# Three edits to a fused attention, gating and token-mixing kernel on one Trainium2 core: last output chunk in two single PSUM banks, ninth blocks' group third, strided operands loaded at earlier steps

## The chip, the cores and the metric

One Trainium2 chip, one core of it. The metric is the device time of one launch in microseconds (us), the median of several runs, lower being better. Engines are named as in the profile: PE is TensorE, DVE VectorE, ACT ScalarE, POOL GpSimd, and SP the engine that issues almost all DMAs.

## The reference

Four batches of 576 rows go through three stages, all with float32 inputs and outputs.

```python
# 1. attention, 8 heads of 64; heads 0-3 local, heads 4-7 strided
scores = q @ k.T / 8
mask_local   = (rel >= 0) & (rel < 32)
mask_strided = (rel >= 0) & (pos_k % 32 == pos_q % 32)
x = softmax(where(mask, scores, -1e9)) @ v          # -> [4, 576, 512]
# 2. spatial gating
h = relu(x @ w_in); u, v = h[..., :512], h[..., 512:]
v_n = (v - mean(v)) / sqrt(var(v) + 1e-6)
x = (u * (w_spatial @ v_n + b_spatial)) @ w_out
# 3. mixing by angles
theta = x @ w_theta
y = w_tok_r @ (x * cos(theta)) + w_tok_i @ (x * sin(theta))
u = x + y
out = u + relu(u @ w_ch)
```

## The kernel before, in words

The matrix products of stages 2 and 3 run in float16 in three passes (high by high, high by low, low by high), over 128x128 weights and 288 columns, two such halves per tile of 128x576. For each batch the main chain is: `v` (240 products in all), its mean and variance (tile `rs` on DVE), the normalised `vn`; `u`; `sp` (the spatial product, which reads `vn`); `x`, the product with `w_out`; `th`, the product with `w_theta`; `z_chunk`, which turns an angle tile of PSUM into sines and cosines (tile `ta`, on ACT and DVE) and has them transposed by DMA into `zf`; `y`, the product with the token weights; `c`, the last product. Generators (`main_v`, `main_mid`, `main_end`) issue it in pieces.

PSUM has three two-bank tiles for this chain (pool `ps_m`, `bufs=3`, function `pm`, line 202) and two single banks, `sc` and `av` (pool `ps_a`, function `pa`, line 205), for attention. A product that wants a fourth `pm` tile waits until the oldest has been read: of the four angle tiles of a batch, the last waits for the reads of the first.

Attention of batches 0 to 2 is computed in float32 in nine groups of score blocks (list `groups`, line 423): a local group holds up to four blocks of 64 rows by 96 keys, one further local group holds the ninth block of both local head pairs, and four strided groups hold six (the last four) blocks of 64 by 64. A group goes through steps: scores on PE into `sc` (`gr_scores`), shift by the maximum on DVE (`gr_shift`, `TENSOR_REDUCE st<-sc`, `TENSOR_TENSOR sm<-sc,st`), exponential on ACT (`gr_exp`), transposes (`gr_turn`), product with the values (`gr_pv`), transposes back and copies into `xT` as a float16 pair (`gr_out`, ACT for the high part, DVE for the low part). Batch 0 runs alone at the start (`attention0`), each group in a pair of banks (`at`, or `sc` and `av`), four pairs in rotation. Batches 1 and 2 (`attention1`, line 661) run beside the main chain of the batch before, one step at a time. Batch 3 (`attention`) uses float16.

In `attention1` a table `loads` (line 680) says after which step's scores the operands of the strided head pairs are loaded: `load_a` loads queries and keys into `kt`, the buffer that a local pair used, and `load_b` loads the values. SP issues all of them in one queue.

Weights arrive as float64 and are made into float16 pairs on the way: a staging buffer is filled by DMA, ACT and DVE form a float32 (`ACTIVATE zf<-zf`, `ACTIVATE wx<-zf`, `SCALAR_TENSOR_TENSOR wx<-zf,wx`), ACT copies the high part (`wtok<-wx`), POOL subtracts for the low part. The token weights (`tok_part`) come in five pieces, i = 0, 2, 4, 6, 8, through two staging buffers in turn, `xT` and `zf`, so that a piece is loaded when the piece two before it has left the buffer. `w_spatial`'s last rows and the bias (`sp_tail`, tile `wspt`) are scaled by ACT and DVE.

In the main chain and in attention of batches 1 to 3 a scheduler sets the order of instructions on each engine by its own costs, from program order with some operations (`ha`, `hv`) put 200 places forward; each engine, and SP's queue, then runs its list in that order.

The end of the last batch (`main_end`, line 989): output chunks 2 and 3 get a `pm` tile each; the last three products of chunk 3 are done for the left half and then for the right half of the columns, each followed by a relu on ACT, an add on DVE and a store.

Of the kernel before, what the change touches and what calls it, by code (L numbers as in the profile page):

```python
# [17 lines left out]
AF = mybir.ActivationFunctionType  # L18
# [9 lines left out]
PS = WS * XS  # L28
# [37 lines left out]
def kernel(  # L66
# [24 lines left out]
    class Pinned:  # L91


        def __init__(self, name):
            self.name, self.engine = name, getattr(tc.nc, name)
# [24 lines left out]
    B, DM, S = out.shape  # L120
    P = 128
# [4 lines left out]
    HS = S // 2  # L126
# [18 lines left out]
    hv, ha, hg = Ahead(nc.vector, AHEAD), Ahead(nc.scalar, AHEAD), Ahead(nc.gpsimd, AHEAD)  # L145
# [56 lines left out]
    def pm(name):  # L202
        return ps_m.tile([P, 2, 512], F32, tag="pm", name=name)

    def pa(tag):
        return ps_a.tile([P, 512], F32, tag=tag, name=tag)
# [4 lines left out]
    def halves(ps):  # L211
        return ps[:, :, 0:HS]

    def fold(ap):
        return ap.rearrange("p (a c) -> p a c", a=2)
# [197 lines left out]
    def spans_of(u):  # L413
        spans = []
        for i, hp, blk, r0, R, o, t0 in pv_blocks(u):
            if spans and spans[-1][0] == hp:
                spans[-1][3] += R
            else:
# [1 line left out]
        return spans  # L420

    QB, CB = 64, 54
    groups = [(True, [(hp, blk) for blk in range(b0, b0 + 4)]) for hp in range(2) for b0 in (0, 4)]
    groups += [(True, [(0, 8), (1, 8)]),
               (False, [(2, i) for i in range(6)]), (False, [(2, i) for i in range(6, 11)] + [(3, 10)]),
               (False, [(3, i) for i in range(6)]), (False, [(3, i) for i in range(6, 10)])]
    NG = len(groups)

    def load_qk(b, hp, q, k, c0, c1, by=None):
        by = by or nc.sync  # L430
        local = hp < 2
        src = kzl[b, hp] if local else kzs[b, hp - 2]
        k0, k1 = (c0 + STRIDE if c0 else 0, c1 + STRIDE) if local else (c0, c1)
        by.dma_start(q[:, c0:c1], qp[b, hp][:, c0:c1])
        for j in range(2):
            h = slice(64 * j, 64 * j + 64)
            by.dma_start(k[h, k0:k1], src[h, j, k0:k1])
# [104 lines left out]
    def gr_exp(g, sm):  # L542
        n = len(groups[g][1]) * (96 if groups[g][0] else QB)
        nc.scalar.activation(sm[:, 0:n], sm[:, 0:n], AF.Exp, scale=0.125)
# [116 lines left out]
    def attention1(b):  # L661
        q, k, v = {}, {}, {}

        def load_a(hp):
            q[hp], k[hp] = kts[hp % 2][:, 0], kts[hp % 2][:, 1]
            load_qk(b, hp, q[hp], k[hp], 0, S)

        def load_b(hp):
            v[hp] = att_p.tile([P, 9, VW], F32, tag="vT", name="v32", bufs=2)
            if hp < 2:  # L670
                load_vl(b, hp, v[hp])
            else:
                load_vs(b, v[hp][:, 0:6].unsqueeze(1), (hp,))

        load_a(0)
        load_b(0)
        yield
        load_a(1)
        load_b(1)
        loads = {4: (load_a, 2), 6: (load_b, 2), 7: (load_b, 3)}  # L680
        un, xs = {}, {}
        for s in range(NG + 3):
            if s < NG:
                sm = att_p.tile([P, 384], F32, tag="sm", name="sm", bufs=2)
                pT = att_p.tile([P, 4, P], F32, tag="pT", name="pT32", bufs=2)
                st = att_p.tile([P, 2, 6], F32, tag="st", name="st", bufs=4)
                un[s] = (sm, pT, st)
            if s >= 3:
                gr_out(b, s - 3, xs.pop(s - 3), pa("sc"))
            if 2 <= s < NG + 2:  # L690
                sm, pT, st = un.pop(s - 2)
                pv = pa("av")[:, 0:3 * VW].rearrange("p (i n) -> p i n", i=3)
                gr_pv(s - 2, v, pT, pv, st, pT)
                xs[s - 2] = pT
            if s < NG:
                sm, pT, st = un[s]
                sc = pa("sc")
                gr_scores(s, q, k, sc)
                gr_shift(s, sc, sm, st)
                gr_exp(s, sm)  # L700
            if s in loads:
                f, hp = loads[s]
                f(hp)
                if s == 4:
                    load_a(3)
            if 1 <= s <= NG:
                sm, pT, st = un[s - 1]
                gr_turn(s - 1, sm, pa4("av"), pT)
            yield
# [279 lines left out]
    def main_end(b):  # L989

        def tok_evac(m, ps):
            x = x2f[:, m, :]
            hv.scalar_tensor_tensor(fold(x), halves(ps), 1.0 / WS, fold(x), op0=ALU.mult, op1=ALU.add)
            split((x2h[:, 0, m, 0:S], x2h[:, 1, m, 0:S]), x, H[E_YLO[m + 4 * (b > 0)]], E_YHI[m + 4 * (b > 0)])

        for m in range(NC):
            ps = pm(f"y{m}")
            rounds = [(i, PASS) for i in range(NZ)]
            if m == 0 and b == B - 1:

                rounds = [(i, ((0, 0), (0, 1))) for i in range(NZ)] + [(i, ((1, 0),)) for i in range(NZ)]
            for k, (i, passes) in enumerate(rounds):
                for n, (ze, we) in enumerate(passes):
                    mm2(ps, zz[:, i, ze, m * P:(m + 1) * P], wtok[:, we, i, :],
                        k == 0 and n == 0, k == len(rounds) - 1 and n == len(passes) - 1)
                if k == len(rounds) - 1:
                    tok_evac(m, ps)
                if k % 3 == 2:
                    yield


        for m0 in (0, 2):
            tiles = [pm(f"c{m0 + i}") for i in range(2)]
            for cs in ((0, 1, 2), (3,)):
                for i in range(2):
                    m = m0 + i
                    o = s1("o") if cs[0] == 3 else None
                    parts = ((0,), (1,)) if cs[0] == 3 and m == NC - 1 and b == B - 1 else ((0, 1),)
                    for a in parts:
                        for c in cs:  # L1020
                            for n, (we, xe) in enumerate(PASS):
                                mm2(tiles[i], wch[:, we, c, m * P:(m + 1) * P], x2h[:, xe, c, :],
                                    c == 0 and n == 0, c == NC - 1 and n == 2, part=a)
                        if cs[0] == 3:
                            f = slice(a[0] * HS, (a[-1] + 1) * HS)
                            h = slice(a[0], a[-1] + 1)
                            ha.activation(fold(o)[:, h], halves(tiles[i])[:, h], AF.Relu, scale=1.0 / PS)
                            hv.scalar_tensor_tensor(o[:, f], x2f[:, m, f], 1.0 / XS, o[:, f], op0=ALU.mult, op1=ALU.add)
                            nc.sync.dma_start(out[b, m * P:(m + 1) * P, f], o[:, f])
                    yield  # L1030


    def switch():
        early[0] = False
# [44 lines left out]
    l0, a0, b0, c0, e0 = win_steps(1, 0)  # L1079
# [115 lines left out]
```

## Time and profile before

| | |
|---|---|
| median of 3 runs | 504.88 us |
| lowest and highest | 504.08, 508.08 us |
| the profiled execution, its own time | 506.96 us |
| span from its first to its last instruction | 505.1 us |
| PE busy in that span | 485.1 us (96%) |
| DVE, ACT, POOL busy | 284.8, 267.8, 92.9 us |

PE is busy for nearly the whole span, so the time is PE's work plus the short stretches in which PE stands still. The views to read are therefore those of PE's waits and, around each wait, the timeline of the other engines. The clock that the throttle granted to PE is given per stretch, 1.00 being full speed (2.4 GHz) and 0.50 half.

### The profile page before, as it was taken

To read this page: it belongs to the slowest core of one execution; us is meant where nothing else is said; L and a number is where in the kernel's file an instruction comes from. 1 tells how busy PE (TensorE), PEld (TensorE's weight loads), DVE (VectorE), ACT (ScalarE), POOL (GpSimd) and SP (SyncE) were. 2 spreads that over 40 slices of the span, in tenths; PEclk is the share of its full clock that TensorE was granted. 3 is DMA by queue.
4 is the path that set the end of the run, shared out by engine and by line. 5 is a ranking of instruction groups with operands and counts; after the bars stand their busy time and mean duration, and the time that the engine had idled before them with its cause. 6 is when DMAs were issued, how large, how long until landed. Compare 5 with 4: busy or idle time off the path is not lost. (4 is left out here: it accounts for less than half of the span.)

```text
span 505.1 us, 10834 instructions
## 1 busy us (share of the span) xinstructions
PE 485.1 (96%) x4460; PEld 364.4 (72%) x4460; DVE 284.8 (56%) x607; ACT 267.8 (53%) x475; POOL 92.9 (18%) x91
## 2 busy tenths in 40 slices
PE   7889989998999999999999989999999999999996
PEld 5655757776567777888758867777657777777774
DVE  3765986555699343473499578772587121227412
ACT  2657788587994233345672757754862022149202
POOL 2042147225124400021003210021005200210220
PEclk9999999999899999999999999999999999999999
DMA  6868748377691024221080156230160020003402
GB/s 177 279 203 234 260 151 270 103 185 225 188 223 49 1 66 150 72 80 27 1 185 4 31 128 195 47 60 5 38 151 1 1 95 1 0 2 80 111 1 93
DMA packets 71788, 52.72 MB, mean 104 GB/s; under 512 B 50552, under 2 KB 59960, under 8 KB 71738
## 3 DMA queue, kind: packets, MB, share of 16 engines
q1 hardware_dynamic: 71434, 51.42, 36.5%
q8 instruction: 35, 0.57, 0.5%
q10 hardware_dynamic: 304, 0.61, 0.4%
q14 instruction: 15, 0.12, 0.1%
HBM read 35.36 MB, written 4.72 MB: 79 GB/s over the span
## 5 line engine op out<-in xcount | busy, mean ns | idle before, releaser
L103 PE MATMUL y<-wtok,zf 128*128 128x288 f16 x864 | 107.2, 286 | 1.0 <-DMA zf<-vn 1.0
L103 PEld LDWEIGHTS <-zf 128*128 128x128 f16 x864 | 84.1, 98 | 23.5 <-DMA zf<-vn 1.3
L103 PE MATMUL sp<-wsp,vn 128*128 128x288 f16 x384 | 52.2, 286 | 1.6 <-ACT vn L103 1.3
L103 PE MATMUL c<-x2h,wch 128*128 128x288 f16 x384 | 49.3, 286 | 2.3 <-ACT o L103 2.3
L103 PE MATMUL th<-x2h,wth 128*128 128x288 f16 x384 | 49.6, 291 | 2.0 <-DVE ta L103 2.0
L103 PE MATMUL x<-zf,wout 128*128 128x288 f16 x384 | 49.9, 286 | 0.0
L103 PE MATMUL u<-xT,win 128*128 128x288 f16 x384 | 49.7, 286 | 0.0
L103 PE MATMUL v<-win,xT 128*128 128x512 f16 (+1 forms) x240 | 48.4, 380 | 0.8 <-DVE xT L103 0.6
L103 PEld LDWEIGHTS <-vn 128*128 128x128 f16 x416 | 39.7, 98 | 12.1 <-ACT vn L103 1.4
L103 POOL TENSOR_TENSOR x2h<-x2f,x2h 128x576 f16<-128x576 f32 x20 | 25.5, 1279 | 119.1 <-ACT x2h L103 47.2
L103 PEld LDWEIGHTS <-wth 128*128 128x128 f16 x384 | 38.1, 100 | 12.5 <-issue 2.2
L103 PEld LDWEIGHTS <-wch 128*128 128x128 f16 x384 | 37.3, 98 | 11.8 <-issue 2.7
L103 PEld LDWEIGHTS <-win 128*128 128x128 f16 x384 | 37.3, 98 | 9.2
L103 PEld LDWEIGHTS <-wout 128*128 128x128 f16 x384 | 36.7, 98 | 9.6
L103 PEld LDWEIGHTS <-xT 128*128 128x128 f16 (+1 forms) x240 | 21.0, 100 | 25.2 <-issue 2.2
L103 ACT ACTIVATE x2h<-x2f 128x576 f16<-128x576 f32 (+1 forms) x28 | 20.9, 746 | 28.9 <-DVE x2f L103 28.4
L103 DVE SCALAR_TENSOR_TENSOR x2f<-y,x2f 128x576 f32<-128x576 f32 x16 | 12.0, 753 | 30.6 <-PE y L103 30.5
L103 DVE TENSOR_TENSOR u<-u,sp 128x576 f32<-128x576 f32 x16 | 12.0, 752 | 28.2 <-PE sp L103 28.2
L103 ACT ACTIVATE o<-c 128x576 f32<-128x576 f32 (+1 forms) x17 | 10.4, 616 | 32.1 <-PE c L103 31.8
L103 DVE TENSOR_TENSOR ta<-ta,x2f 128x1152 f32<-128x1152 f32 x16 | 21.5, 1354 | 9.8 <-ACT ta L103 9.8
L103 POOL TENSOR_TENSOR zf<-u,zf 128x576 f16<-128x576 f32 x8 | 10.7, 1340 | 86.0 <-ACT zf L103 86.0
L103 DVE TENSOR_TENSOR vn<-ta,vn 128x1152 f16<-128x1152 f32 x16 | 21.5, 1355 | 5.6 <-ACT vn L103 5.6
(140 smaller groups left out, 738.2 us busy)
## 6 DMA issues: line engine op xcount, KB each, us to landing
out_dram<-o SPq DMA_DIRECT2D x15, 288.0 KB
kt<-in_qp_dram SPq DMA_DIRECT2D x8, 288.0 KB
qs<-in_qd_dram SPq DMA_DIRECT2D x8, 288.0 KB
x2f<-in_w_in_dram SPq DMA_DIRECT2D x2, 1024.0 KB
zf<-in_w_in_dram SPq DMA_DIRECT2D x2, 1024.0 KB
xT<-in_w_ch_dram SPq DMA_DIRECT2D x2, 1024.0 KB
kt<-in_kzl_dram SPq DMA_DIRECT2D x8, 152.0 KB
ks<-in_kl_dram SPq DMA_DIRECT2D x4, 304.0 KB
```

The lines of the kernel that those rows point to most:

```text
L103: ins = f(*args, **kwargs)
```

## The change

Three edits. First, the list of groups is reordered: the group of the two ninth blocks, which stood fifth, stands third, behind both groups of head pair 0. Second, with head pair 0 done two steps sooner and pair 1 at the fifth step as before, the table of loads is moved: pair 2's queries and keys after step 2 instead of 4, pair 3's still after step 4 but by an entry of their own, pair 2's values after step 5 instead of 6, pair 3's after step 6 instead of 7. Third, the last output chunk of the last batch is held in the two single banks `sc` and `av` through a small class `Banks`, and its two relus read one bank each.

```diff
--- before.py
+++ after.py
@@ -420,10 +420,10 @@
         return spans
 
     QB, CB = 64, 54
-    groups = [(True, [(hp, blk) for blk in range(b0, b0 + 4)]) for hp in range(2) for b0 in (0, 4)]
-    groups += [(True, [(0, 8), (1, 8)]),
-               (False, [(2, i) for i in range(6)]), (False, [(2, i) for i in range(6, 11)] + [(3, 10)]),
-               (False, [(3, i) for i in range(6)]), (False, [(3, i) for i in range(6, 10)])]
+    groups = [(True, [(0, i) for i in range(4)]), (True, [(0, i) for i in range(4, 8)]), (True, [(0, 8), (1, 8)]),
+              (True, [(1, i) for i in range(4)]), (True, [(1, i) for i in range(4, 8)]),
+              (False, [(2, i) for i in range(6)]), (False, [(2, i) for i in range(6, 11)] + [(3, 10)]),
+              (False, [(3, i) for i in range(6)]), (False, [(3, i) for i in range(6, 10)])]
     NG = len(groups)
 
     def load_qk(b, hp, q, k, c0, c1, by=None):
@@ -677,7 +677,7 @@
         yield
         load_a(1)
         load_b(1)
-        loads = {4: (load_a, 2), 6: (load_b, 2), 7: (load_b, 3)}
+        loads = {2: (load_a, 2), 4: (load_a, 3), 5: (load_b, 2), 6: (load_b, 3)}
         un, xs = {}, {}
         for s in range(NG + 3):
             if s < NG:
@@ -701,8 +701,6 @@
             if s in loads:
                 f, hp = loads[s]
                 f(hp)
-                if s == 4:
-                    load_a(3)
             if 1 <= s <= NG:
                 sm, pT, st = un[s - 1]
                 gr_turn(s - 1, sm, pa4("av"), pT)
@@ -1011,6 +1009,8 @@
 
         for m0 in (0, 2):
             tiles = [pm(f"c{m0 + i}") for i in range(2)]
+            if m0 and b == B - 1:
+                tiles[1] = Banks(pa("sc"), pa("av"))
             for cs in ((0, 1, 2), (3,)):
                 for i in range(2):
                     m = m0 + i
@@ -1024,11 +1024,21 @@
                         if cs[0] == 3:
                             f = slice(a[0] * HS, (a[-1] + 1) * HS)
                             h = slice(a[0], a[-1] + 1)
-                            ha.activation(fold(o)[:, h], halves(tiles[i])[:, h], AF.Relu, scale=1.0 / PS)
+                            ps = tiles[i][0:P, a[0], 0:HS].unsqueeze(1) if len(a) == 1 else halves(tiles[i])
+                            ha.activation(fold(o)[:, h], ps, AF.Relu, scale=1.0 / PS)
                             hv.scalar_tensor_tensor(o[:, f], x2f[:, m, f], 1.0 / XS, o[:, f], op0=ALU.mult, op1=ALU.add)
                             nc.sync.dma_start(out[b, m * P:(m + 1) * P, f], o[:, f])
                     yield
 
+
+    class Banks:
+
+
+        def __init__(self, *banks):
+            self.banks = banks
+
+        def __getitem__(self, key):
+            return self.banks[key[1]][key[0], key[2]]
 
     def switch():
         early[0] = False
```

The scheduler gives the engines other orders after this. Three places are shown; the names are those of the section on the kernel, a number behind a name tells buffers apart.

DVE after the first batch's attention, in the chain of the variance of batch 0's `v`: `rs` is that chain, `vr` its result, `wspt` the tail of the spatial weights, `st` and `sm` the third group of batch 1's attention. Before:

```order
L103 TENSOR_REDUCE st<-sc 128x4
L103 SCALAR_TENSOR_TENSOR rs<-rs 128x5
L103 SCALAR_TENSOR_TENSOR wspt<-x2f,wspt 64x576
L103 TENSOR_TENSOR rs<-rs 128x5
L103 TENSOR_TENSOR sm<-sc,st 128x384
L103 TENSOR_TENSOR rs<-rs 128x5
L103 SCALAR_TENSOR_TENSOR wspt<-x2f,wspt 1x576
L103 SCALAR_TENSOR_TENSOR rs<-rs 128x5
```

The same stretch now:

```order
L103 TENSOR_REDUCE st<-sc 128x2
L103 SCALAR_TENSOR_TENSOR rs<-rs 128x5
L103 SCALAR_TENSOR_TENSOR wspt<-x2f,wspt 64x576
L103 TENSOR_TENSOR rs<-rs 128x5
L103 TENSOR_TENSOR sm<-sc,st 128x192
L103 TENSOR_TENSOR rs<-rs 128x5
L103 SCALAR_TENSOR_TENSOR rs<-rs 128x5
```

The third group is the small one (192 columns instead of 384), and the one-row `wspt` has left the chain; it stands now behind the first `vn` of 64 rows.

ACT in batch 0, at the last piece of the token weights (`xT_94<-xT_94 128x576`) and the first angle tiles (`ta<-th`). Before:

```order
L103 ACTIVATE xT_94<-xT_94 128x576
L103 ACTIVATE wtok<-wx 128x1152
L103 ACTIVATE wx<-xT_94 128x576
L103 ACTIVATE ta_1549<-th_1493 128x576
L103 ACTIVATE ta_1566<-th_1494 128x576
```

The same stretch now:

```order
L103 ACTIVATE xT_94<-xT_94 128x576
L103 ACTIVATE wx<-xT_94 128x576
L103 ACTIVATE ta_1549<-th_1493 128x576
L103 ACTIVATE ta_1566<-th_1494 128x576
L103 ACTIVATE wtok<-wx 128x1152
```

The copy of the piece before (`wtok<-wx`) has moved from ahead of the angle tiles to behind them. Further up on ACT the first piece's `wtok<-wx` and the third piece's `xT_94<-xT_94` have moved the other way, the one behind the first read of an `x` tile, the other ahead of the last.

PE at the same place: batch 2's first score group (`sc<-kt`) and the angle products. Before:

```order
L103 MATMUL th_1577<-x2h,wth 128x288
L103 MATMUL sc<-kt_80 64x96 x8
L103 LDWEIGHTS identb
L103 MATMUL sc<-mask_100,identb 128x96
L103 LDWEIGHTS identb
L103 MATMUL sc<-mask_100,identb 128x288
L103 LDWEIGHTS wth
L103 MATMUL th_1613<-x2h,wth 128x288
```

Where the score group stands now:

```order
L103 MATMUL y_1899<-wtok,zf 128x288
L103 MATMUL sc<-kt_80 64x96 x8
L103 LDWEIGHTS identb
L103 MATMUL sc<-mask_100,identb 128x96
L103 LDWEIGHTS identb
L103 MATMUL sc<-mask_100,identb 128x288
L103 LDWEIGHTS zf
L103 MATMUL y_1899<-wtok,zf 128x288
```

The group stood between the third and the fourth angle tile; it has moved into the products of `y`, and the four angle tiles follow one another without it. From the later part of batch 1's main chain on, the orders of PE, ACT and DVE are the same as before up to the last output chunk.

## Rows read from the trace of the kernel before

**Rows 1.** Page, part 1: busy us, share of the span, instructions.

```profile
PE 485.1 (96%) x4460; PEld 364.4 (72%) x4460; DVE 284.8 (56%) x607; ACT 267.8 (53%) x475; POOL 92.9 (18%) x91
```

**Rows 2.** Waits of PE: who for whom, us in total, times, longest.

```profile
PE at L103 <- DVE xT L103: 2.7, 3, 1.1
PE c L103 <- ACT o L103: 2.3, 2, 1.7
PE th L103 <- DVE ta L103: 2.0, 1, 2.0
PE at L103 <- DMA kt<-in_kzl_dram: 1.7, 1, 1.7
...
PE sp L103 <- ACT vn L103: 1.3, 1, 1.3
```

**Rows 3.** Windows: length, busy us by engine, clock, DMA.

```profile
200.00:225.00 25.00, 25.00 (x302) 19.90 (x300) 14.19 (x29) 10.44 (x21) 2.79 (x4) 1.00 0.30 86
```

**Rows 4.** Timeline, batch 0's attention: start, us, instruction, idle before, releaser.

```profile
28.68 0.23 ACT L103 ACTIVATE xT<-at 128x64 f16<-128x64 f32 x1 [0.29 <-DVE xT L103]
```

**Rows 5.** Timeline, variance chain and its readers; a 192-column shift.

```profile
58.02 0.55 DVE L103 TENSOR_REDUCE st<-sc 128x4 f32<-128x384 f32 x1
...
59.30 0.54 DVE L103 TENSOR_TENSOR sm<-sc,st 128x384 f32<-128x384 f32 x1
...
60.16 0.75 DVE L103 SCALAR_TENSOR_TENSOR wspt<-x2f,wspt 1x576 f16<-1x576 f32 x1 [0.25 <-ACT wspt L103]
...
61.74 2.36 DVE L103 TENSOR_SCALAR vr<-vr,mv,rs 128x512 f32<-128x512 f32 x5
...
64.86 0.42 PE L103 MATMUL sp<-wsp,vn 128*128 128x288 f16 x2 [1.26 <-ACT vn L103]
...
77.21 0.36 DVE L103 TENSOR_TENSOR sm<-sc,st 128x192 f32<-128x192 f32 x1
```

**Rows 6.** Timeline, the angle weights: second load, POOL, first use.

```profile
74.61 0.37 SPq L103 DMA_DIRECT2D x2f<-in_w_th_dram  x1
...
85.53 2.28 POOL L103 TENSOR_TENSOR wth<-x2h,wth 128x512 f16<-128x512 f32 x2
...
112.83 4.22 PE L103 MATMUL th<-x2h,wth 128*128 128x288 f16 x33
```

**Rows 7.** Timeline, last token piece and first angle tiles.

```profile
121.25 0.73 ACT L103 ACTIVATE xT<-xT 128x576 f32<-128x576 f32 x1 [1.65 <-DMA xT<-in_w_ti_dram]
121.89 1.16 ACT L103 ACTIVATE wtok<-wx 128x1152 f16<-128x1152 f32 x1
...
122.56 0.88 PE L103 MATMUL sc<-kt 64*64 64x96 f32 x16
122.94 0.72 ACT L103 ACTIVATE wx<-xT 128x576 int32<-128x576 uint8 x1
123.57 0.62 ACT L103 ACTIVATE ta<-th 128x576 int32<-128x576 f32 x1
...
125.73 4.66 PE L103 MATMUL th<-x2h,wth 128*128 128x288 f16 x24 [2.02 <-DVE ta L103]
```

**Rows 8.** Windows: while `x` is read, and behind PE's wait.

```profile
102.80:111.90 9.10, 9.10 (x92) 7.03 (x91) 5.17 (x12) 8.29 (x14) 1.19 (x1) 1.00 0.63 143
125.73:129.15 3.42, 3.42 (x16) 2.14 (x16) 2.39 (x4) 2.95 (x4) 1.52 (x2) 0.53 0.81 285
```

**Rows 9.** Timeline, the last output chunk.

```profile
499.70 0.95 ACT L103 ACTIVATE o<-c 128x576 f32<-128x576 f32 x2 [4.49 <-PE c L103]
...
500.71 0.53 PE L103 MATMUL c<-x2h,wch 128*128 128x288 f16 x3 [0.67 <-ACT o L103]
...
501.06 0.45 DVE L103 SCALAR_TENSOR_TENSOR o<-x2f,o 128x288 f32<-128x288 f32 x1
...
501.27 0.41 ACT L103 ACTIVATE o<-c 128x288 f32<-128x288 f32 x1 [0.61 <-PE c L103]
501.71 0.46 DVE L103 SCALAR_TENSOR_TENSOR o<-x2f,o 128x288 f32<-128x288 f32 x1 [0.20 <-ACT o L103]
```

## The prediction

> **What bounds the kernel now.** I read the page's busy times first, then the waits of PE, then the windows, then the timeline around each wait. PE is busy 485.1 of 505.1 us [rows 1], so the whole prize is 20 us of standing still, including the start and the last store; in the middle, as from 200 to 225 us, PE has no idle time at all at full clock [rows 3]. The waits name the rest [rows 2]: 2.7 us in three pieces behind DVE's copies in batch 0's attention, 2.3 us behind ACT's output relus (0.67 of it in the last chunk, the remainder in batch 1's output, which the change leaves alone), 2.0 us at the angle tiles, 1.7 us for the first load, 1.3 us before the spatial product. No row shows PE waiting for a load of `kt` or of values after the first 1.7 us. An edit can help here only by shortening one of these waits, and it can hurt anywhere, since PE has no spare time elsewhere. So I price the edits wait by wait and not by work: the same blocks are scored, shifted and multiplied after as before.
>
> **Last output chunk.** PE's last three products begin at 500.71, 0.67 us late, because the relu of the left half reads the same tile [rows 9]. With two tiles that wait goes. What is late next: ACT finishes the left half's relu at 499.70 + 0.95 = 500.65, so the right half's relu can start there and not at 501.27, and is over 0.41 us later, at 501.06. DVE then is the limit: its add of the left half runs from 501.06 to 501.51, so the right half's add starts at 501.51 and not at 501.71 [rows 9]. The gain is 0.20 us; the store behind it, from 502.17 to the end of the span at 505.1, is unchanged. Bounds: 0.6 if DVE overlapped fully, 0 if ACT's relus need more time between banks. I take -0.2.
> The Trainium skill (PSUM — Partial Sum Buffer, section "PSUM bank collisions raise a hardware error") says that engines need guarding by bank, and that a matmul may run beside a read of a different bank. By that rule the halves, in two banks before too, never needed the wait, and all 0.67 us would come off; the rows above leave 0.2, because DVE is behind it.
>
> **Batch 0's attention.** The group with two short copies per engine moves from the fifth step to the third. Such a pair goes in turns: ACT's second copy waited 0.29 us for DVE's first and took 0.23 [rows 4]. Before, this turn-taking ended just ahead of one of the three waits for DVE; now it stands ahead of an earlier one, with an exponential and a transposed copy behind it on ACT. One turn, 0.5 us, is added there, and the step that had it loses it; the step made small at the third place leaves PE a little idle, too, and the fifth is larger. I take +0.2, bounds -0.5 (one wait of about 0.9, a third of 2.7, half gone) and +0.7.
>
> **The variance chain.** This is where the new third group helps. From DVE's reduction at 58.02 to the first `vr` at 61.74 the chain `rs` is interleaved with batch 1's third group. That group is now half as wide: its shift takes 0.36 instead of 0.54, and for the reduction I take the same 0.36 against 0.55; together 0.37 us less. The one-row `wspt`, 0.75 us and a wait of 0.25 before it, leaves the chain: 1.00 us. So `vr` and the `vn` that ACT makes of it come 1.37 us earlier [rows 5]. PE waited 1.26 us for that `vn`, having arrived at 63.60 [rows 5]. It now arrives about 0.4 sooner, since a half-size score group (the full one took 1.15 us up to 123.71 [rows 7]) stands ahead; that work is done later, not saved. Operands at 64.86 - 1.37 = 63.49, PE at about 63.2: a wait of 0.3 is left, 0.9 is gained. Bounds: 1.3 (all of it) and 0 (the low part of `vn`, which has the `wspt` ahead of it now, stops PE two products later). I take -0.9.
>
> **The loads.** Keys, queries and values move forward in SP's queue past weight loads, so these pay. The second load of the angle weights left SP at 74.61 and POOL finished its parts at about 87.8 [rows 6]; behind thirteen value loads and three of keys and queries, at about the 0.37 us that one issue takes, it is some 6 us later. The first angle product is at 112.83 [rows 6], so 25 us cover it, and I cost it at nothing. The earlier operands save nothing either, since nobody waited for them.
>
> **The angle tiles.** The largest single wait of the trace: PE stands still for 2.02 us before 125.73, because the first angle tile must be read before the fourth can be written [rows 7], and PE then ran for 3.42 us at a granted clock of 0.53, mostly its lower level of 1.2 GHz [rows 8], which cost 3.42 x 0.47 = 1.6 us more. ACT is what is late: it waited 1.65 us for the last token piece, converted it at 121.25, copied the piece before for 1.16 us, made `wx` and only at 123.57 read the first tile [rows 7]. Now that copy stands behind the angle tiles: the read comes 1.16 us sooner. But batch 2's score group, which filled PE from 122.56 to 123.71, has moved into `y`: PE arrives 1.15 us sooner. The two cancel; the wait stays at about 2.0 us and with it the half-speed stretch, and I take 0. Bounds: -3.6 (2.02 + 1.6, all gone) and +1.8, from ACT's new order further up. While `x` is read, ACT was busy for 8.29 of 9.10 us [rows 8], 0.81 free; a `wtok` copy of 1.16 and a conversion of twice 0.73 (twice the half-size one of rows 7) come into that stretch, 2.62 us, so it ends up to 1.8 late. I take the middle because the load of the last piece, whose landing sets the chain, has no change in its order against its own predecessor.
> The Trainium skill (TensorE: Matmul & The Clock Gate, section "Part 1: The HAM clock gate") says that the cold stretch of one kernel differs from run to run. By that rule 1.6 us could be there or not in any execution, with or without the change. The one profiled execution cannot show it.
>
> **The sum.** -0.2 + 0.2 - 0.9 + 0 + 0 = -0.9 us. Against the profiled execution, 506.96 us by its own time, 505.1 of it the span, that gives 506.1. The median of the three runs is 504.88, 2.1 us below the profiled execution; the terms are waits that do not depend on this offset, so the median would go to 504.0.
>
> **Rivals.** First, the wait at the angle tiles closes. For it: 1.16 us off ACT's chain, and the small third group gives every chain of batch 0 a start of a microsecond; against it: PE arrives 1.15 sooner. If it goes with the half-clock stretch, 504.0 - 3.6 = 500.4. Chance 0.2.
> Second, slower: ACT's backlog. The conversions of the first and third token piece stand between the reads of `x` now; once they cost ACT more than its 0.81 us of slack, the last `x` and all behind it on ACT are late, up to the angle tiles, and PE waits there for 2.0 + 1.8 us. The 0.9 gained before is then waited away as well, since the chain of token pieces and not PE decides when the fourth angle tile starts: 504.88 - 0.2 + 0.2 + 1.8 = 506.7. For it: ACT's 91% in that stretch; against it: the copy moved behind the angle tiles and 1.65 us of ACT waiting. Chance 0.2.
> Third, the edits change the order and nothing else: loads that nobody waited for, and the gain before `sp` waited away at the angle tiles. Only the tail and batch 0's attention are left, -0.2 + 0.2: 504.9. Chance 0.15.
> The forecast, between 502.8 and 505.0, keeps 0.45.
>
> **How the numbers follow.** The forecast alone spans 502.8 to 505.0 by its small bounds. The range for 8 in 10 must take in the first rival at 500.4 and the second at 506.7: 500.2 to 507.0. One per cent of 504.88, 5.05 us, is about what a measurement of this kernel can tell from no change. Faster than 499.8 needs the first rival and most of the other small waits: 0.08. Slower than 509.9 needs the second and a further wait of 3 us in a stretch where PE has none now: 0.04. Within: 0.88.
>
> **What would show it.** In the profile after: no wait of PE for `o` in the last chunk, and the right half's add directly behind the left's. The wait of `sp` for `vn` at 0.3 us or less, at about 63.5 us. At the angle tiles a wait of PE of about 2 us and a stretch of half clock behind it; none of either would be the first rival, nearly 4 us the second, together with ACT reading the last `x` tile over a microsecond after PE has finished it. New waits of PE between 70 and 110 us, where there are hardly any now, would make the prediction wrong in a way that none of the cases has, and would point to the moved loads.

## The result, and the profile after

The changed kernel takes 512.31 us (median of 4 runs, 510.69 to 515.76); the kernel before, beside it, 504.48 (4 runs). The ratio is 1.0136 [1.0089, 1.0183], the brackets being the 95% interval: slower, above the 509.9 us (1%) that the prediction named as the bound, though the interval begins just under 1%, and outside the range of the prediction. Measured again with the experiments it was 511.40 against 506.16, 1.0093 [1.0062, 1.0125]. Each ratio is to the kernel before measured beside it, since that differs between chips by over 1 us (504.89 and 506.16 below). The profiled execution of the changed kernel took 511.17 us, 509.4 of it the span, against 506.96 and 505.1 before.

Busy times of the engines in the changed kernel, to be read against [rows 1]:

```profile
PE 483.8 (95%) x4460; PEld 364.6 (72%) x4460; DVE 286.8 (56%) x607; ACT 266.9 (52%) x475; POOL 93.3 (18%) x91
```

PE is busy 1.3 us less and the span is 4.3 us longer, so PE stands still for 25.6 us instead of 20.0. The waits of PE say where [rows 2]:

```profile
PE sc L103 <- DVE sm L103: 5.0, 2, 4.3
...
PE sp L103 <- DVE vn L103: 2.5, 1, 2.5
...
PE c L103 <- ACT o L103: 1.4, 1, 1.4
...
PE sp L103 <- ACT vn L103: 0.4, 1, 0.4
...
PE th L103 <- DVE ta L103: 0.2, 1, 0.2
```

`sp` for DVE's `vn` is new, 2.5 us at once. `sc` for `sm` was one wait of 0.7 us before, at 56 us; it is still there, and a second one of 4.3 us has joined it. Two have shrunk as one hopes: `sp` for ACT's `vn` from 1.3 to 0.4, `th` for `ta` from 2.0 to 0.2. `c` for `o` has lost the 0.67 us of the last chunk, and some of the rest. By stretches, before (window; length, then busy us of PE, its loads, DVE, ACT, POOL; granted clock; DMA):

```profile
55.00:75.00 20.00, 16.77 (x171) 12.35 (x170) 17.73 (x42) 15.66 (x23) 6.02 (x4) 1.00 0.54 186
...
120.00:135.00 15.00, 12.98 (x87) 7.88 (x85) 8.35 (x11) 12.26 (x18) 6.25 (x4) 0.89 0.72 194
155.00:175.00 20.00, 20.00 (x195) 15.91 (x193) 12.93 (x26) 5.99 (x10) 9.88 (x7) 1.00 0.06 16
```

and after:

```profile
0.00:55.00 55.00, 47.04 (x541) 32.85 (x542) 33.93 (x83) 32.38 (x54) 13.98 (x28) 1.00 0.78 232
55.00:75.00 20.00, 16.40 (x146) 11.86 (x145) 17.03 (x43) 13.29 (x20) 5.11 (x5) 0.91 0.60 205
75.00:120.00 45.00, 43.44 (x496) 33.72 (x494) 27.91 (x53) 34.53 (x53) 18.38 (x18) 1.00 0.61 193
120.00:135.00 15.00, 14.78 (x93) 8.93 (x92) 9.87 (x11) 14.79 (x22) 5.00 (x4) 1.00 0.71 208
155.00:175.00 20.00, 15.67 (x145) 12.10 (x141) 11.34 (x26) 6.70 (x9) 7.30 (x5) 0.91 0.05 15
```

Length less PE's time is its idle time. The two stretches of before that are left out have 6.99 (to 55 us) and 0.42 us of it (75 to 120). So the change is +0.97, +0.37, +1.14, -1.80 and +4.33 us from the first stretch to the last; the stretch between, 135 to 155 us, has none before or after, and what follows 175 us adds 0.6. The sixth column behind the length shows the clock: the stretch of half clock that stood behind the angle tiles is gone (0.89 to 1.00 from 120 to 135 us), and two others have come, at 55 to 75 and at 155 to 175 us.

The spatial product, in the timeline of after, against [rows 5]:

```profile
62.32 0.65 POOL L103 COPY k<-vn 64x512 f16<-64x512 f16 x1 [10.32 <-ACT vn L103]
62.54 0.99 DVE L103 TENSOR_TENSOR vn<-vr,vn 64x512 f16<-64x512 f32 x1
63.26 0.42 PE L103 MATMUL sp<-wsp,vn 128*128 128x288 f16 x2 [0.37 <-ACT vn L103]
63.55 0.75 DVE L103 SCALAR_TENSOR_TENSOR wspt<-x2f,wspt 1x576 f16<-1x576 f32 x1
64.23 2.12 POOL L103 TENSOR_TENSOR vn<-vr,vn 128x1024 f16<-128x1024 f32 x1 [1.26 <-ACT vn L103]
64.34 3.10 DVE L103 TENSOR_TENSOR vn<-vr,vn 128x1024 f16<-128x1024 f32 x1
67.49 0.66 PE L103 MATMUL sp<-wsp,vn 128*128 128x288 f16 x4 [2.46 <-DVE vn L103]
```

The wait for the high part is 0.37 us at 63.26. Then PE needs the low part, and DVE's subtraction takes 3.10 us. In the kernel before the same two subtractions read so:

```profile
65.70 1.22 DVE L103 TENSOR_TENSOR vn<-vr,vn 128x1024 f16<-128x1024 f32 x1
65.83 3.09 POOL L103 TENSOR_TENSOR vn<-vr,vn 128x1024 f16<-128x1024 f32 x1 [1.26 <-ACT vn L103]
```

There DVE began 0.13 us before POOL, took 1.22 us, and POOL took 3.09. After, POOL begins 0.11 us before DVE, takes 2.12, and DVE takes 3.10. PE reads DVE's half first. The 2.46 us are not all a loss: of the waits of before in this stretch, 0.89 us of the 1.26 for the high part, 0.54 for `pT` at 65.93, 0.34 for POOL's half at 68.97 and 0.26 for `xT` at 70.38 are gone, so that PE stands only 0.37 us longer from 55 to 75 us. The half clock behind the long wait comes on top.

From 75 to 120 us there are two waits of PE over 0.5 us, where the kernel before has none:

```profile
83.25 0.34 PE L103 MATMUL sc<-mask,identb 128*128 128x384 bf16 x1 [0.60 <-DMA v<-in_vs_dram]
...
108.56 0.41 PE L103 MATMUL av<-ident,sm 128*128 128x128 f32 x2 [0.67 <-DVE pT L103]
```

The first is put down to a load of values, in the second execution of the change to DVE (0.65 us at 82.94).

Batch 2's first two score groups, in the timeline of after:

```profile
154.46 0.88 PE L103 MATMUL sc<-kt 64*64 64x96 f32 x16
...
161.93 1.22 DVE L103 TENSOR_TENSOR vn<-vr,vn 128x1024 f16<-128x1024 f32 x1
...
163.06 0.55 DVE L103 TENSOR_REDUCE st<-sc 128x4 f32<-128x384 f32 x1
...
164.35 1.47 PE L103 MATMUL sc<-kt 64*64 64x96 f32 x16 [4.33 <-DVE sm L103]
```

The first group is scored at 154.46, in the middle of the token product, and occupies the tile `sc`. Its maximum comes on DVE only at 163.06, 8.6 us later, behind batch 1's whole variance chain, `vr` and `vn`, with DVE busy all that time; the second group's scores wait for the tile for 4.33 us.

The angle tiles, timeline of after, against [rows 7]:

```profile
122.51 1.16 ACT L103 ACTIVATE ta<-th 128x576 int32<-128x576 f32 x2
...
123.57 1.15 ACT L103 ACTIVATE wtok<-wx 128x1152 f16<-128x1152 f32 x1
124.11 3.10 PE L103 MATMUL th<-x2h,wth 128*128 128x288 f16 x24 [0.22 <-DVE ta L103]
```

The two windows of [rows 8] in the changed kernel:

```profile
102.80:111.90 9.10, 8.43 (x86) 6.62 (x85) 5.19 (x8) 7.59 (x13) 3.03 (x2) 1.00 0.63 166
125.73:129.15 3.42, 3.42 (x23) 2.03 (x21) 0.59 (x1) 3.39 (x6) 1.59 (x2) 1.00 1.03 382
```

ACT's first read of an angle tile is 1.06 us sooner than in [rows 7], the copy of `wtok` stands behind it, and full clock follows. ACT's load while `x` is read is 7.59 of 9.10 us.

The last chunk, timeline of after, against [rows 9]:

```profile
503.91 0.65 ACT L103 ACTIVATE o<-c 128x576 f32<-128x576 f32 x1 [4.49 <-PE c L103]
504.07 0.53 PE L103 MATMUL av<-x2h,wch 128*128 128x288 f16 x3
...
504.59 1.50 DVE L103 SCALAR_TENSOR_TENSOR o<-x2f,o 128x576 f32<-128x576 f32 x3 [4.39 <-ACT o L103]
...
505.80 0.88 SPq L103 DMA_DIRECT2D out_dram<-o  x2
```

PE's last three products no longer wait, and DVE's three adds run back to back up to 506.09. Counted from where the products end if they do not wait (before: 500.71 - 0.67 + 0.53 = 500.57; after: 504.60), it is 1.49 us instead of 1.60 to the last add, but 4.80 instead of 4.53 to the end of the span: SP is still issuing its last two stores, 0.88 us from 505.80, until 0.6 us after the last add. The rows for batch 0's pair turn [rows 4] and the angle weights [rows 6] have their like at 22.69 us (0.23 us, 1.21 of waiting) and at 83.51 and 95.65 us (the load and POOL's second part); no product of theta waits for weights.

### The profile page after: what moved, and what is told of

Its sections match the earlier page's. It is cut to its first block, busy times and chain, and to the rows that moved or that the text cites. A ratio compares the mean times of both kernels' runs of the same rounds, so it can differ in the third digit from the quotient of the medians.

```text
span 509.4 us, 10835 instructions
## 1 busy us (share of the span) xinstructions
PE 483.8 (95%) x4460; PEld 364.6 (72%) x4460; DVE 286.8 (56%) x607; ACT 266.9 (52%) x475; POOL 93.3 (18%) x91
## 5 line engine op out<-in xcount | busy, mean ns | idle before, releaser
L103 PE MATMUL th<-x2h,wth 128*128 128x288 f16 x384 | 48.2, 286 | 0.2 <-DVE ta L103 0.2
L103 PE MATMUL c<-x2h,wch 128*128 128x288 f16 x360 | 46.2, 286 | 1.4 <-ACT o L103 1.4
L103 ACT ACTIVATE o<-c 128x576 f32<-128x576 f32 x15 | 9.7, 644 | 30.6 <-PE c L103 30.3
```

Of the source, the lines that this page charges most:

```text
L103: ins = f(*args, **kwargs)
```

## The experiments

Two theories were on trial. One says that the loss lies in the two new waits, and that each has its own cause: who starts first of DVE and POOL, and where the earlier loads let the scheduler put batch 2's first group. The rival says that the regrouping or the earlier loads cost by themselves, or that a wait removed comes back further on.

**The last chunk alone.** The kernel before with the two banks and nothing else.

> Only the last output chunk in two single banks, all else as before. Both theories: the right half's relu starts about 0.6 us sooner, DVE's add right behind that of the left half, so the end comes 0.2 us sooner, and no wait of PE elsewhere changes; the time is within 1% of before. Were the tail a part of the loss, PE would wait in the last chunk.

Measured in one run: 507.23 us, beside a median of 504.89 of the kernel before; its granted clock was 0.996. No wait in the last chunk; 4.71 us from the last product to the end of the span. Kernels that keep the old tail have 4.53, 4.60 and 4.59 (before twice, and the experiment on the loads), those with the new one 4.80, 4.71 and 4.78 (after, this one, and the next). So the edit removes PE's wait of 0.67 us, and the kernel ends 0.1 to 0.3 us later all the same, where 0.2 us sooner was expected.

**The groups without the loads.** The whole change, but the table of loads as before:

```diff
-        loads = {2: (load_a, 2), 4: (load_a, 3), 5: (load_b, 2), 6: (load_b, 3)}
+        loads = {4: (load_a, 2), 6: (load_b, 2), 7: (load_b, 3)}
```

(and pair 3's operands again right after pair 2's).

> All of the change but the table of loads, which is that of before. Theory A (the loss is two new waits of PE, each with half clock behind it: 2.5 us for the low part of vn, 4.3 us for the second score group of batch 2, whose first group the earlier loads have pushed from the angle products into y): the score group stands among the angle products again, so the wait of 4.3 us and its 1.7 us of half clock are gone; the wait of 2.5 us stays; the wait at the angle tiles of about 2 us comes back, with half clock or without. Time between before and after, some 2 to 4 us under after. Rival B (the reordered groups themselves are the loss, the loads do nothing): as slow as after within 1 us.

Measured: 505.92 us (10 runs), ratio 1.0002 [0.9973, 1.0032]. Waits of PE in its profile:

```profile
PE sp L103 <- DVE vn L103: 2.5, 1, 2.5
...
PE sc L103 <- DVE sm L103: 0.7, 1, 0.7
```

The wait of 4.3 us is gone (the 0.7 that is left for `sm` stands at 56 us, in the kernel before too): batch 2's first group is scored among theta's products again, at 123.33 us. The wait of `sp` for DVE's low part is there as in the change. So that wait comes with the regrouping, and the 4.3 us need the loads (what the loads do alone is below). Two parts of the expectation missed: the wait at the angle tiles came back as 0.75 us (at 125.23) and not about 2, and the time is that of the kernel before and not between the two. The regrouping with the two banks costs nothing that these runs can tell from zero.

**The low part without POOL.** The change, with batch 0's second low part on DVE (one letter for each low part, `v` for DVE, `g` for POOL, the first two those of batch 0):

```diff
-E_VLO = 'vgvg'
+E_VLO = 'vvvg'
```

> The changed kernel, with the low part of batch 0's second vn pair made by DVE in place of POOL. Theory A (POOL began its pass 0.1 us before DVE's and DVE then stood until POOL was through): DVE's pass of 1024 columns takes 1.2 us and not 3.1, PE's wait before the third spatial product falls from 2.5 to 0.6 us or less and no half clock follows it; about 3.5 us under the changed kernel. Rival B (the wait is DVE's list, in which the one-row wspt now stands ahead of that pass): the wait stays at 1.5 us or more, and little is gained.

Measured: 508.63 us (10 runs), ratio to before 1.0070 [1.0044, 1.0096], against 1.0136 and 1.0093 of the change. Timeline:

```profile
63.96 2.36 DVE L103 TENSOR_TENSOR vn<-vr,vn 128x1024 f16<-128x1024 f32 x2
65.24 1.64 PE L103 MATMUL sp<-wsp,vn 128*128 128x288 f16 x12 [0.59 <-DVE vn L103]
```

Two subtractions on DVE one after the other, 2.36 us, are done sooner than one that stands behind POOL's, 3.10. Of the 2.46 us, 1.87 were POOL; the 0.59 that stay are less than the 0.75 us of the moved `wspt` ahead on DVE, which no run took away. No half clock follows. 0.88 us come back at 71.51 us. The wait of 4.37 us for the scores stays, at 160.94. The interval of the ratio overlaps those of the change, so it is the trace and not the time that shows this repair.

**Batch 2's attention later.** The change, with the scheduler's (the "planner's") start for batch 2's steps five of its units later, so that the first group is scored after 162 products of `y` and not after 126:

```diff
-ATT_AT = (None, (2.7, 3.9), (79.0, 5.4), (169.9, 4.6))
+ATT_AT = (None, (2.7, 3.9), (84.0, 5.4), (169.9, 4.6))
```

> The changed kernel, with batch 2's attention begun 5 us later, so that its first score group stands behind 162 products of y and not behind 126. Theory A (its shift stands on DVE behind the chain of the variance anyway, and the next group waits for it): PE's wait of 4.3 us falls under 0.5 and the half clock behind it goes; 5 to 6 us under the changed kernel. Rival B (DVE is short of time in that stretch whatever the order): a wait of 2 us or more stays there, or comes a group later.

Measured: 506.07 us (10 runs), ratio to before 1.0025 [1.0004, 1.0046]. Timeline:

```profile
157.67 0.88 PE L103 MATMUL sc<-kt 64*64 64x96 f32 x16
...
162.47 0.55 DVE L103 TENSOR_REDUCE st<-sc 128x4 f32<-128x384 f32 x1
...
163.75 0.88 PE L103 MATMUL sc<-kt 64*64 64x96 f32 x16 [0.52 <-DVE sm L103]
```

DVE takes the maximum 0.6 us sooner than in the change, PE comes 3.2 us later to the first group and finds work until the tile is free. The wait of `sp`, 2.47 us, stays, and in this execution no half clock stood behind it. By the ratios, with the change at 1.0093 to 1.0136, the groups without the loads gain 4.6 to 6.8 us on it, the low part without POOL 1.2 to 3.3 and the later attention 3.4 to 5.6, where 2 to 4, about 3.5 and 5 to 6 were expected.

**The change again, and both repairs together,** on one chip, with the next.

> The changed kernel again, beside the next two, for a second median. Both theories (the wait of spatial product for the low part of vn, and the second score group of batch 2 behind DVE's chain) expect the two waits in the same places: sp 2.3 to 2.6 us at about 67 us, sc 4.2 to 4.5 us at about 164 us, whatever the execution. The loss against before is then 4 to 8 us, with the half-clock stretches (0 to 2 of them, 1.7 us each) as the scatter. Rival (the first measurement was inflated by a bad chip or bad runs): within 2 us of before, with the same waits.

> The change with both repairs: second low part of vn on DVE and not on POOL, and batch 2's attention begun 5 us later in the planner's time. Theory (the two waits are the whole loss): sp wait 0.6 or less at 65 us, sc wait 0.6 or less at 164 us, no wait of 2 us at the angle tiles, so PE waits some 6 us less than in the changed kernel; time 503 to 505, and 1 to 2 below before only if nothing new opens. Rival (each wait closed comes back further on, as the single repairs left 0.5 to 1 us at 71 us and 2.5 us near 300 us): 505.5 to 507, with a new or longer wait named behind 170 us.

Measured: the change 511.40 us (9 runs), ratio 1.0093 [1.0062, 1.0125], with `sp` waiting 2.47 and `sc` 4.32 us: both waits are the same to 0.01 us in two executions. With both repairs 504.44 us (12 runs), ratio to before 0.9956 [0.9927, 0.9985]: faster than both kernels, by 7 and by 1.7 us. Windows of its profile (span 501.4):

```profile
120.00:135.00 15.00, 14.90 (x86) 7.77 (x85) 10.81 (x12) 14.73 (x20) 4.41 (x3) 1.00 0.72 183
...
155.00:175.00 20.00, 19.21 (x189) 14.92 (x188) 11.23 (x21) 8.62 (x13) 7.60 (x5) 1.00 0.10 30
```

The angle tiles cost 0.1 us of idle time instead of 2.02, the stretch from 155 us 0.79 instead of 4.33. The rival is right in a small part: 0.89 us at 71.64 come back. A wait of 0.67 at 105.32, which the kernel before does not have either, is that of the change at 108.56 and stays with both repairs.

**The loads without the groups.** The kernel before with the new table of loads alone. Without the regrouping, pair 2's operands are loaded over pair 0's while pair 0's ninth block is still to come, so in batches 1 and 2 that block is computed from operands of pair 2. The amount of work is the same, but that block now depends on this load, which it does in no other kernel here.

> The kernel before with only the table of loads changed (no regrouping, no two banks in the last chunk). Theory: the earlier loads alone move batch 2's first score group out of theta into the token product, so the wait of the second group for DVE's shift is there, 4.0 to 4.6 us at about 163 us, and the angle wait of 2.0 us is gone or under 0.5; the second row block of wspt also stands behind vr here, so POOL starts the low part of vn before DVE and the spatial product waits 2 to 3 us for DVE's part near 67 us; time 508 to 512. Rival (loads and regrouping are needed together): neither wait over 1 us, time 504 to 506.

Measured: 508.00 us (median of 12 runs, one of them of 2550 us), ratio 1.0028 [1.0000, 1.0056]. Timeline:

```profile
64.25 1.23 DVE L103 TENSOR_TENSOR vn<-vr,vn 128x1024 f16<-128x1024 f32 x1
64.39 3.09 POOL L103 TENSOR_TENSOR vn<-vr,vn 128x1024 f16<-128x1024 f32 x1 [0.79 <-ACT vn L103]
...
65.54 0.91 PE L103 MATMUL sp<-wsp,vn 128*128 128x288 f16 x6 [0.72 <-DVE vn L103]
...
161.85 1.42 PE L103 MATMUL sc<-kt 64*64 64x96 f32 x16 [2.05 <-DVE sm L103]
```

Half of the expectation held: the earlier loads alone move the first group into the token product and open the wait for `sm`, and the wait at the angle tiles is gone. It is 2.05 us and not over 4, because DVE takes the maximum 2.5 us sooner here, at 160.56. The other half failed, and tells more: the one-row `wspt` stands behind `vr` here too, but DVE began the low part 0.14 us before POOL, and PE waited 0.72 us instead of 2.46. One difference stands a step earlier: in the change DVE came 0.22 us after POOL's copy of `k` (62.32 and 62.54 above) and took 0.99 us for the small `vn`; here it came 0.03 us before POOL and took 0.69, and POOL's copy 1.12 instead of 0.65. The kernel before lost that step too (63.92 and 64.20, 0.91 us), but had no `wspt` behind it and was still 0.13 us ahead at the low part. So by these traces it takes both, the lost step and the moved `wspt`; no run changes one of them alone.

The loads alone cost 0.28% and the rest of the change 0.02%, the two together 0.93 to 1.36%. The extra shows as waits: 2.46 us for `vn` and not 0.72, 4.33 for `sm` and not 2.05, because DVE takes the maximum 2.5 us later. Why it does so with the regrouping was not tried.

**DVE and POOL alone.** A kernel of single instructions on data already loaded. In the first, DVE and POOL subtract 128x1024 each, in both orders.

> Only subtractions of 128x1024, f16 out of f32 less f16, on DVE and on POOL, four times each way: POOL alone, DVE alone, POOL first and DVE 0.1 to 0.3 us behind, DVE first and POOL behind; the output is zeros and none of the reference is computed. Theory (the two engines take turns at whole instructions: the first to start runs, the other stands until it is through): alone DVE 1.1 to 1.3 us and POOL 2.0 to 2.2; POOL first: POOL 2.0 to 2.2, DVE 3.0 to 3.3; DVE first: DVE 1.1 to 1.3, POOL 3.0 to 3.3. Rival (they share bandwidth and slow each other): both longer than alone in both orders, whichever starts first, each by a third or more. Second rival (the 3.1 us came from somewhere else in the kernel): each as alone in both orders.

```profile
11.70 1.23 DVE L44 TENSOR_TENSOR lo_d<-src_d,hi_d 128x1024 f16<-128x1024 f32 x1 [0.46 <-ACT hi_d L38]
11.71 3.19 POOL L41 TENSOR_TENSOR lo_p<-src_p,hi_p 128x1024 f16<-128x1024 f32 x1 [2.16 <-ACT hi_d L38]
```

Alone DVE took 1.23 us and POOL 2.12. Where POOL was meant to be first, ACT wrote its operand 0.09 us before DVE's, and DVE still began 0.01 us before it: POOL begins 0.14 to 0.15 us behind the end of ACT's write here, DVE 0.03 to 0.04. So DVE was first in all eight pairs, 1.22 to 1.23 us, and POOL took 3.00 to 3.19. The other order was not tried by this run. In the second kernel POOL was given a lead:

> Only single instructions; the output is zeros and none of the reference is computed. POOL's subtraction of 128x1024 is started well before one DVE instruction (0.5 us or more), twice for each of four forms of it: two operands of SBUF, one operand and two scalars, a maximum over one operand, one operand of PSUM and one of SBUF; each also alone. Theory (the first to start runs, an instruction of the other with two operands of SBUF stands until it is through): two operands alone 1.2 us and behind POOL its own 1.2 plus what is left of POOL's 2.1, 2.6 to 3.2 in all, POOL at 2.1. The other forms read SBUF with one operand only: by the kernel's trace, where such ran beside POOL, each as alone, POOL at 2.1 or slightly over. Rival (they share bandwidth): POOL is stretched too, by a third or more, in every pair. Second rival (every DVE instruction stands behind POOL): all four forms end after POOL does.

The lead came out at 2 us, so POOL was nearly through when DVE began, and every instruction took its time alone: this run tells nothing apart. The third has a smaller lead:

> The single instructions of the last run again, with DVE's instruction begun about 0.4 us and about 0.8 us after POOL's and not just at its end; the output is zeros and none of the reference is computed. Theory (the first to start runs, an instruction of DVE with two operands of SBUF stands until it is through): two operands alone 1.2 us, behind POOL 2.9 to 3.1 at the gap of 0.4 and 2.5 to 2.7 at 0.8, POOL 2.1 both times; one operand and two scalars (0.81 alone), the maximum over one operand (1.22) and one operand of PSUM with one of SBUF (0.69) as alone. Rival (they share bandwidth): POOL over 2.6 and DVE under 2.4 for two operands. Second rival (every DVE instruction stands behind POOL): all four forms take their time alone plus 1.3 to 1.8.

```profile
9.66 2.12 POOL L47 TENSOR_TENSOR lo_p<-src_p,hi_p 128x1024 f16<-128x1024 f32 x1 [7.97 <-ACT hi_p L39]
9.98 2.88 DVE L51 TENSOR_TENSOR lo_d<-src_d,hi_d 128x1024 f16<-128x1024 f32 x1 [1.12 <-ACT src_d L39]
...
19.57 2.35 DVE L53 TENSOR_SCALAR vr<-src_d,st 128x1024 f32<-128x1024 f32 x1 [0.95 <-ACT src_d L39]
...
28.29 1.22 DVE L55 TENSOR_REDUCE st<-src_d 128x4 f32<-128x1024 f32 x1 [1.09 <-ACT src_d L39]
...
35.79 0.69 DVE L57 TENSOR_TENSOR lo_s<-ps,src_d 128x512 f32<-128x512 f32 x1 [0.85 <-ACT src_d L39]
```

POOL keeps its 2.12 us; DVE's subtraction, begun 0.32 us behind it, takes 2.88, and a later one 2.41. The start of POOL plus its 2.12 plus about 1.1 gives DVE's end: DVE stands until POOL is through. A maximum over one operand (1.22) and a subtraction that reads one operand from PSUM (0.69) run beside POOL in their time alone. The expectation missed one form: one operand with two scalars, 0.81 alone, stands too (2.35 and, in the second pair, 1.88).
The Trainium skill (SBUF — State Buffer, section "Who interferes with whom") says this: DVE and GpSimd share a pair of ports that whoever starts first holds for the whole instruction; a DVE instruction with two operands in SBUF, or a copy or `tensor_scalar` in a two-port mode, needs it, a reduction does not. These rows agree with it.

**The kernel before once more,** for its clock.

> The kernel before once more, for a second profile. Theory (a wait of about 2 us brings half clock in some executions and none in others): the angle wait is there again, 1.6 to 2.1 us near 126 us, and the half-clock stretch of 3.4 us stands behind it or behind another wait of over 1 us, or nowhere; the waits for DVE's and ACT's operands come back within 0.3 us of the first profile, those for loads within 0.7. Rival (the clock falls at this wait every time): half clock from 126 to 129 us again.

Its windows over the stretch at the angle tiles and at the spatial product:

```profile
126.48:129.58 3.10, 3.10 (x25) 2.44 (x25) 2.39 (x4) 2.63 (x4) 1.20 (x2) 1.00 0.77 267
66.59:69.90 3.31, 3.31 (x17) 2.29 (x16) 2.89 (x2) 2.82 (x5) 2.65 (x1) 0.55 0.00 0
```

PE waited 1.70 us for the angle tile, and ran at full clock behind it; half clock stood from 66.6 to 69.9 us, behind the waits for `vn`, and from about 8 to 15 us. In the experiment on the last chunk, whose order there is that of the kernel before, a wait of 1.66 us at the angle tile was followed by full clock as well.

## Why the prediction was wrong

**Last chunk** (-0.2, bounds 0 and -0.6): the wait went as forecast, and DVE's adds run back to back. The step "the store behind it, from 502.17 to the end of the span, is unchanged" failed: SP's last two stores are issued one behind the other until 0.6 us after the last add (before, 0.4), and the end is 0.1 to 0.3 us longer. Small, but of the other sign.

**Batch 0's attention** (+0.2, bounds -0.5 and +0.7): idle time up to 55 us is 6.99 us before, 7.96 and 6.88 in two executions of the change, with 1.7, 2.3 and 1.8 of it the first loads. The term cannot be told from nothing.

**The variance chain** (-0.9, bounds 0 and -1.3): the step itself came out to 0.1 us. `sp` waits 0.37 us for the high part, at 63.26, where 0.3 at 63.5 was said. What failed is the bound "0 (the low part of `vn` ... stops PE two products later)": it put no price on the low part. The `wspt` copy that left the head of the chain stands ahead of DVE's low part, which then came 0.11 us after POOL's instead of 0.13 before, and stood behind it for 1.9 us. 0.59 + 1.87 = 2.46 us were added where 0.89 were gained; with the smaller waits that went, the stretch has 0.37 us more of idle time and not 0.9 less, and half clock besides. The trace of before held the price: POOL's 3.09 us in it were a subtraction of 2.12 that stood behind DVE's. The prediction did not ask why it took that long.

**The loads** (0): the angle weights come 8.9 us later, 83.51 instead of 74.61 us for the load, where 6 were said, and pay nothing, as forecast. What failed is that their effect on the scheduler's order was priced only at the angle tiles. The score group that "has moved into `y`" was counted as 1.15 us of PE's work moved, and not by whom its result is taken up there: DVE, with 8.6 us of its list, most of it batch 1's variance chain, ahead of it. That is the 4.33 us, the largest term of all. Putting the loads back removes it, and so, up to 0.52 us, does starting the steps later. The sign that the prediction named for the loads, new waits between 70 and 110 us, came in small: 1.14 us more of idle time from 75 to 120 us, half of it still there with both repairs (PE busy for 44.00 us there, against 44.58 before and 43.44 in the change). What causes these was not tried.

**The angle tiles** (0, bounds -3.6 and +1.8): the first rival happened, in its mechanism and not in its time. ACT's read is 1.06 us sooner, for the 1.16 forecast. The step that failed is "PE arrives 1.15 us sooner": PE comes at 124.11 - 0.22 = 123.89 and not sooner than the 123.71 of before, having stood 2.5 us longer up to 120 us (13.1 against 10.6) and run a stretch at half clock on the way, so nothing cancels. With both repairs PE does come sooner, and finds no wait either: there ACT converts the last token piece at 117.75 and reads the tiles at 119.03. The reason given for the middle of the bounds, that this piece's load sets the chain and does not move, does not hold there. And the half clock of 1.6 us was a property of one execution: the kernel before has the wait and full clock in another.

**The second and third rivals** did not happen: ACT is busy 7.59 of 9.10 us where its backlog was feared, less than the 8.29 before.

**The clock.** The prediction priced half clock at one place. Over the runs of one chip the mean granted clock was 0.9947 before (26 runs) and 0.9888 after (9 runs); times 510 us that is an estimate of 3 us more lost to the clock at most, of the 5.2 us between the medians. Some of it falls where PE stands and costs nothing (in the second execution of the change the clock, 0.83 from 161 to 163 us, fell while PE did nothing), and a straight line through the 26 runs of before gives 0.6 us of time for each us lost by this reckoning, which makes the estimate 1.8 us. The wait for the scores, 4.3 to 4.4 us, was followed by half clock in all three executions that have it, that of 2.5 us for the low part in three of four (with the later attention it has 2.47 us and no half clock behind it).

**The range.** The bounds of the small terms, added, give 502.5 to 505.6 us, and not the 502.8 to 505.0 of the forecast; the time lies far above either. No rival of the prediction had the two waits in it.

What stays open: the wait for ACT's relu near 300 us was between 1.2 and 2.7 us in ten profiles; in one with 2.65 ACT had stood 2.52 us for a load of queries, where it stood 1.25 in one with 1.37, and why that load lands later was not tried. Open too are 1.78 us at 87.55 us that only the loads without the groups showed, and PE's 1.3 us less of busy time.

## What to carry to other kernels

When a step moves, price it by who takes up its result at the new place: a score group moved to another place in PE's list cost 4.33 us here, because DVE's list had a long chain ahead of its maximum. When an instruction in the trace takes half as long again as its like, find out why before counting on the order around it: here 0.1 us decided whether PE waited 2.46 us for DVE's half or 0.34 for POOL's. And a half-clock stretch seen in one execution should be priced at its average over several.

## What was not expected of the hardware

When both subtract with two SBUF operands, DVE and POOL take turns by whole instructions, and the turn goes to whoever starts first, by 0.01 us in the narrowest case: 1.22 us for DVE and 3.09 for POOL in one order, 3.10 and 2.12 in the other. A DVE instruction with one SBUF operand and two scalars is held as well (0.81 to 2.35 us), a maximum is not.
The same wait brings half clock or not from one execution to the next: behind 1.7 to 2.0 us at the angle tiles once in three executions of the same order, behind 2.5 us at the spatial product in three of four. The Trainium skill (TensorE: Matmul & The Clock Gate, section "Part 1: The HAM clock gate") calls the cold stretch at a kernel's start variable from run to run; these rows show the same in the middle of one. The range of the prediction held that variation at one place only.
